# Where a decode kernel's first weights land: wq whole and first, w_down on 128 partitions

## The chip, the cores and the metric

One Trainium2 chip, one of its cores. The time is device time in microseconds (us) of one execution. Before the change it was 2534.05 us, the median of three runs (2532.77 to 2534.06). The core has TensorE (matmuls, called PE in the profile), VectorE (DVE), ScalarE (ACT), GpSimd (POOL), SyncE (SP), which here issues nearly all transfers, and 16 DMA engines that move the data between HBM and SBUF, the on-chip memory of 128 partitions.

## The reference, cut to what matters

One token is decoded. A 32-head attention over a cache of 65,536 positions and a SwiGLU feed-forward read the same input x, and a sigmoid gate mixes their results. Everything is bf16.

```python
def _A_ref(x, k_cache, v_cache, wq, wo):          # x [1,1,512], caches [1,32,65536,128]
    q = (x @ wq).reshape(B, Sq, H, Dh).transpose(0, 2, 1, 3)
    scores = jnp.einsum("bhqd,bhkd->bhqk", q, k_cache) * (Dh ** -0.5)
    p = softmax(scores, axis=-1)
    o = jnp.einsum("bhqk,bhkd->bhqd", p, v_cache)
    return o.transpose(0, 2, 1, 3).reshape(B, Sq, H * Dh) @ wo

def _B_ref(x, w_gate, w_up, w_down):              # F = 1792
    return (silu(x @ w_gate) * (x @ w_up)) @ w_down

g = sigmoid((x * gate_w).sum(-1, keepdims=True))
return g * _A_ref(...) + (1 - g) * _B_ref(...)
```

The caches are 2 x 32 x 65536 x 128 x 2 bytes, 1073.7 MB. wq and wo have 4.19 MB each, w_gate, w_up and w_down 1.835 MB each.

## The kernel before, in words

A head's K and V are cut into G = 4 tiles of 128 partitions with 128 rows of 128 numbers each (NB = 128), so a tile has 32 KB in every partition, 4 MB in all. There are N = 128 tiles of K and as many of V.

**The ring.** All large loads go into five slots of 32 KB per partition (SLOTS = 5). `take` (line 81) hands out the slot that was freed first, `give` (line 88) puts one back. A load into a slot waits until whatever read the slot's last content is done. SP issues the loads in program order, so a load that waits holds up those behind it in SP's queue. The slots lie in SBUF behind the pool of constants; as built, the first begins at byte 30,976 of each partition.

**The scores.** `products` (line 245) multiplies a K tile by the head's query on VectorE (line 254) and folds it by halves (line 258), to 64 numbers a row for the first head (FIRST) and to 32 for the others (WIDTH). `scores` (line 263) sums the rest on TensorE with identity matmuls (line 267), which frees the K slot; `fold` (line 277) takes the last four numbers together. At a head's end come the row maximum (line 285), the exponentials (line 294), and `values` (line 316), 32 matmuls for a V tile (line 322), which frees the V slot.

**The queries.** `queries(g)` (line 146) makes the queries of four heads with four matmuls against wq (line 149) and copies them to SBUF on ScalarE (line 156).

**The beginning, written out by hand (lines 99 to 124 and 380 to 420).** SP first issues the first four heads' part of wq (0.5 MB, rows of 1 KB) into a tile of the `wo_pool`, then K0, K1 and K2. The other 3.5 MB of wq (rows of 7 KB) have the fourth slot. A one-element GpSimd copy (line 381) writes into that slot once the first queries are done, and the load waits for it:

```python
queries(0)
nc.gpsimd.tensor_copy(out=wq_t[0:1, 0:1], in_=q_bc[0:1, 0:1])
nc.sync.dma_start(out=wq_rest, in_=wq_rows[:, :, QW:])
```

K0's slot then takes w_gate and w_up, with K3 issued between them (lines 387 to 389). K1's slot takes w_down, K2's takes V0, and wq's takes K4. w_down lies on 64 partitions, 28 KB in each, and comes in eight transfers of 8 partitions (line 402), six ahead of K4 and two behind it:

```python
firsts = (0, 1, 2, 3, 32, 33, 34, 35)
part = slice(firsts[i], firsts[i] + 29, 4)
```

**The loop (line 433).** From n = 4 on, each step loads one K tile and one V tile, multiplies and sums K tile n and weights V tile v. The list `steps` lets V fall behind K by up to LAG = 8 tiles after n = 40. In step n = 4 the feed-forward is finished (`feed_forward_mid`, line 214, and `feed_forward_out`, line 223): since w_down lies on 64 partitions, two matmuls (line 227) turn the hidden vector from 128 x 14 to 64 x 28, ScalarE copies it (line 231), and 28 matmuls of 512 columns (line 233) follow. Then w_down's slot is free for K6.

**The end.** The last V tile comes in six pieces, and half of wo in four (line 169), behind it in SP's queue.

Of the kernel before, what the change touches and what calls it, by code (L numbers as in the profile page):

```python
# [8 lines left out]
ACT = mybir.ActivationFunctionType  # L9
ALU = mybir.AluOpType  # L10
AXIS = mybir.AxisListType
P = 128
# [3 lines left out]
NB = 128  # L16
# [17 lines left out]
def kernel(  # L34
# [14 lines left out]
    nc = tc.nc  # L49
    bf16 = mybir.dt.bfloat16  # L50
    f32 = mybir.dt.float32

    _, H, Sk, Dh = A_k_cache.shape
    D = A_x.shape[2]
    F = B_w_gate.shape[1]
    KT = D // P
    FT = F // P
    G = Sk // (NB * P)
    NBH = Sk // P
    N = H * G  # L60
    QG = 4
# [3 lines left out]
    consts = ctx.enter_context(tc.tile_pool(name="consts", bufs=1))  # L65
# [3 lines left out]
    wo_pool = ctx.enter_context(tc.tile_pool(name="wo_pool", bufs=2))  # L69
# [3 lines left out]
    psum_m = ctx.enter_context(tc.tile_pool(name="psum_m", bufs=2, space=bass.MemoryType.PSUM))  # L73
# [7 lines left out]
    def take(name):  # L81
        slot = free.pop(0)
        held[name] = slot
        return ring.tile(
            [P, NB * Dh], bf16, name=name.split(".")[0], tag=f"slot{slot}"
        )

    def give(name):
        free.append(held.pop(name))

    xT = consts.tile([P, KT], bf16, name="xT")
    gwT = consts.tile([P, KT], bf16, name="gwT")
    with nc.allow_non_contiguous_dma(reason="small"):
# [1 line left out]
        nc.scalar.dma_start(out=gwT, in_=gate_w.rearrange("(p t) -> p t", t=KT))  # L95

    QW = QG * Dh
    wq_rows = A_wq.rearrange("(p t) f -> p t f", t=KT)
    wq_first = wo_pool.tile([P, KT, QW], bf16, name="wq_first", tag="wo_sb")
    nc.sync.dma_start(out=wq_first, in_=wq_rows[:, :, :QW])  # L100

    K_tiles, V_tiles, S_tiles, F_tiles, P_tiles, O_tiles = {}, {}, {}, {}, {}, {}

    def load(dst, cache, n, name, cuts=(0, NB), slot=None):
        h, g = divmod(n, G)
        t = take(f"{name}.{n}") if slot is None else slot
        view = t.rearrange("p (j d) -> p j d", d=Dh)
        src = cache[0, h, g * NB * P : (g + 1) * NB * P, :].rearrange("(p j) d -> p j d", j=NB)
        for a, b in zip(cuts[:-1], cuts[1:]):
            nc.sync.dma_start(out=view[:, a:b, :], in_=src[:, a:b, :])  # L110
        dst[n] = view

    def load_k(n):
        load(K_tiles, A_k_cache, n, "K_t")
# [1 line left out]
    def load_v(n):  # L116
        load(V_tiles, A_v_cache, n, "V_t", V_CUTS.get(N - n, (0, NB)))

    load_k(0)
    load_k(1)  # L120
    load_k(2)
    wq_t = take("wq_t.0")
    wq_rest = wq_t[:, : KT * (H * Dh - QW)].rearrange("p (t f) -> p t f", t=KT)
    K3_t = take("K_t.3")

    ident_f = consts.tile([P, P], f32, name="ident_f")
    make_identity(nc, ident_f[:])
    ident_b = consts.tile([P, P], bf16, name="ident_b")
# [4 lines left out]
    q_bc = consts.tile([P, H * Dh], bf16, name="q_bc")  # L133
# [12 lines left out]
    def queries(g):  # L146
        qg_ps = psum_m.tile([P, QW], f32, name="qg_ps", tag="misc")
        for t in range(KT):
            nc.tensor.matmul(
                qg_ps,  # L150
                lhsT=X_bc[:, t, :],
                rhs=wq_first[:, t, :] if g == 0 else wq_rest[:, t, (g - 1) * QW : g * QW],
                start=(t == 0),
                stop=(t == KT - 1),
            )
        nc.scalar.activation(out=q_bc[:, g * QW : (g + 1) * QW], in_=qg_ps, func=ACT.Copy)
# [34 lines left out]
    def gate_sum():  # L191
        xg = consts.tile([P, KT], f32, name="xg")
        nc.vector.tensor_tensor(out=xg, in0=xT, in1=gwT, op=ALU.mult)
        xs = consts.tile([P, 1], f32, name="xs")
        nc.vector.tensor_reduce(out=xs, in_=xg, axis=AXIS.X, op=ALU.add)
        return xs

    def gate_exp(xs):
        g_ps = psum_m.tile([P, 1], f32, name="g_ps", tag="misc")
        nc.tensor.matmul(g_ps, lhsT=ones_f, rhs=xs, start=True, stop=True)  # L200
        eg2 = consts.tile([P, 1], f32, name="eg2")
        nc.scalar.activation(out=eg2, in_=g_ps, func=ACT.Exp, scale=-1.0)
        return eg2

    def gate_value(eg2):
        nc.vector.tensor_scalar_add(eg2, eg2, 1.0)
        nc.vector.reciprocal(gval, eg2)
        rest = consts.tile([1, 1], f32, name="rest")
        nc.vector.tensor_scalar(
            out=rest, in0=gval[0:1, :], scalar1=-1.0, scalar2=1.0, op0=ALU.mult, op1=ALU.add  # L210
        )
        return rest
# [9 lines left out]

    def feed_forward_out(hT, rest):
        b_ps = psum_m.tile([1, D], f32, name="b_ps", tag="misc")
        h_ps = psum_m.tile([HP, GT], f32, name="h_ps", tag="misc")
        for r in range(2):
            nc.tensor.matmul(
                h_ps[:, r * FT : (r + 1) * FT], lhsT=ident_b[:, r::2], rhs=hT, start=True, stop=True
            )
        h2 = consts.tile([HP, GT], bf16, name="h2")  # L230
        nc.scalar.activation(out=h2, in_=h_ps, func=ACT.Copy)  # L231
        for t in range(GT):
            nc.tensor.matmul(  # L233
                b_ps, lhsT=h2[:, t : t + 1], rhs=wd_sb[:, t, :], start=(t == 0), stop=(t == GT - 1)
            )
        nc.scalar.activation(out=b_sb, in_=b_ps, func=ACT.Copy, scale=rest)
        for i, a in enumerate(a_ps):
            nc.tensor.matmul(  # L238
                a, lhsT=ones_f[0:1, 0:1], rhs=b_sb[:, i * HD : (i + 1) * HD], start=True, stop=False
            )  # L240

    def width_of(n):
        return FIRST if n < G else WIDTH

    def products(n, a=0, b=NB):
        h = n // G
        K = K_tiles[n][:, a:b, :]
        qb = q_bc[:, h * Dh : (h + 1) * Dh]
        q_rep = bass.AP(
            tensor=qb.tensor,  # L250
            offset=qb.offset,
            ap=[list(qb.ap[0]), [0, b - a], [1, Dh]],
        )
        yield nc.vector.tensor_tensor(out=K, in0=K, in1=q_rep, op=ALU.mult)  # L254
        half = Dh
        while half > width_of(n):
            half //= 2
            yield nc.vector.tensor_tensor(  # L258
                out=K[:, :, 0:half], in0=K[:, :, 0:half], in1=K[:, :, half : 2 * half],
                op=ALU.add,  # L260
            )

    def scores(n):
        S = F_tiles[n] = psum_s.tile([P, NB, QUAD], f32, name="S_ps")
        width = width_of(n)
        for c in range(0, width, QUAD):
            nc.tensor.matmul(  # L267
                S,
                lhsT=ident_b,
                rhs=K_tiles[n][:, :, c : c + QUAD],  # L270
                start=(c == 0),
                stop=(c == width - QUAD),
            )
        del K_tiles[n]
        give(f"K_t.{n}")

    def fold(n):
        h, g = divmod(n, G)
        if g == 0:
            S_tiles[h] = small.tile([P, NBH], f32, name="S_sb")  # L280
        nc.vector.tensor_reduce(  # L281
            out=S_tiles[h][:, g * NB : (g + 1) * NB], in_=F_tiles.pop(n), axis=AXIS.X, op=ALU.add
        )
# [90 lines left out]
    def score_tile(n):  # L374
        for _ in products(n):
            pass
        if n:
            fold(n - 1)

    queries(0)  # L380
    nc.gpsimd.tensor_copy(out=wq_t[0:1, 0:1], in_=q_bc[0:1, 0:1])
    nc.sync.dma_start(out=wq_rest, in_=wq_rows[:, :, QW:])
    score_tile(0)
    scores(0)
    gu_t = take("gu_t.0")
    wgu_sb = gu_t[:, : 2 * KT * F].rearrange("p (w t f) -> p w t f", w=2, t=KT)
    nc.sync.dma_start(out=wgu_sb[:, 0], in_=B_w_gate.rearrange("(p t) f -> p t f", t=KT))
    load(K_tiles, A_k_cache, 3, "K_t", slot=K3_t)
    nc.sync.dma_start(out=wgu_sb[:, 1], in_=B_w_up.rearrange("(p t) f -> p t f", t=KT))
    score_tile(1)  # L390
    xs = gate_sum()
    scores(1)
    wd_t = take("wd_t.0")
    HP = P // 2
    GT = F // HP
    wd_sb = wd_t[:HP, : GT * D].rearrange("p (t n) -> p t n", t=GT)
    wd_rows = B_w_down.rearrange("(p t) n -> p t n", t=GT)
    firsts = (0, 1, 2, 3, 32, 33, 34, 35)

    def load_wd(i):  # L400
        part = slice(firsts[i], firsts[i] + 29, 4)
        nc.sync.dma_start(out=wd_sb[part], in_=wd_rows[part])

    for i in range(6):
        load_wd(i)
    for g in range(1, H // QG):
        queries(g)
    give("wq_t.0")
    eg2 = gate_exp(xs)
    load_k(4)  # L410
    load_wd(6)
    load_wd(7)
    score_tile(2)
    rest = gate_value(eg2)
    scores(2)
    load_v(0)
    ff = feed_forward_in()
# [15 lines left out]
    for n, v in steps:  # L433
# [22 lines left out]
        if n == G:  # L456
            hT = feed_forward_mid(*ff)
# [7 lines left out]
        if n == G:  # L465
            feed_forward_out(hT, rest)
            give("wd_t.0")
# [49 lines left out]
```

## Time and profile before

| | |
|---|---|
| median of three runs | 2534.05 us (2532.77 to 2534.06) |
| the profiled execution | 2534.41 us, its span 2532.6 us |
| TensorE busy | 1533.7 us (61%) |
| VectorE busy | 2083.7 us (82%) |
| read from HBM | 1087.64 MB, 429 GB/s over the span |
| a transfer of a K tile | 4096 KB, 35.3 us from issue to landing (median) |
| mean granted TensorE clock | 0.772 of full speed |

The profile page has one execution, in 40 slices of 63.3 us where it shows rates. "DMA share" is the mean busy share of the 16 DMA engines in a stretch; a packet counts with its whole size where it ends, so that over 2 or 3 us the share can pass 1. A row of the timeline has start, length, engine, line, operation, its tiles, and in brackets how long the engine was idle before and what ended that. SPq stands for SP's queue of issues: such a row starts when the issue does, not when data moves. Packet and landing records, where they are named, are the trace's lists of DMA packets (start, length, size) and of the 16 completion counts that each transfer posts, one for each DMA engine.

### The profile page before, as it was taken

To read this page: it belongs to the slowest core of one execution; us is meant where nothing else is said; L and a number is where in the kernel's file an instruction comes from. 1 tells how busy PE (TensorE), PEld (TensorE's weight loads), DVE (VectorE), ACT (ScalarE), POOL (GpSimd) and SP (SyncE) were. 2 spreads that over 40 slices of the span, in tenths; PEclk is the share of its full clock that TensorE was granted. 3 is DMA by queue.
4 is the path that set the end of the run, shared out by engine and by line. 5 is a ranking of instruction groups with operands and counts; after the bars stand their busy time and mean duration, and the time that the engine had idled before them with its cause. 6 is when DMAs were issued, how large, how long until landed. Compare 5 with 4: busy or idle time off the path is not lost.

```text
span 2532.6 us, 13195 instructions
## 1 busy us (share of the span) xinstructions
PE 1533.7 (61%) x5786; PEld 581.6 (23%) x5786; DVE 2083.7 (82%) x744; ACT 77.7 (3%) x208; POOL 0.9 (0%) x7
## 2 busy tenths in 40 slices
PE   4656656665566555555665566556656665665569
PEld 1222222222222112222222122222222221222223
DVE  7788888888887999988888888888888888888860
ACT  1000000000000000000000000000000000000000
POOL 0000000000000000000000000000000000000000
PEclk9777777777777787787777777777777777777779
DMA  9999999999999999999999999999999999999998
GB/s 412 418 431 433 435 432 430 434 433 432 431 433 434 431 433 434 432 431 434 433 432 433 434 432 432 435 431 432 432 434 432 431 435 433 431 434 433 432 432 351
DMA packets 43915, 1088.49 MB, mean 430 GB/s; under 512 B 4753, under 2 KB 9362, under 8 KB 10258
## 3 DMA queue, kind: packets, MB, share of 16 engines
q1 hardware_dynamic: 43570, 1087.65, 99.7%
q8 instruction: 45, 0.74, 0.1%
q14 instruction: 12, 0.10, 0.0%
q10 hardware_dynamic: 288, 0.00, 0.0%
HBM read 1087.64 MB, written 0.00 MB: 429 GB/s over the span
## 4 chain that ended last, share of the span: by engine, by line
DMA 71%; PE 23%; DVE 4%; issue 1%; ACT 0%; SPq 0%; DVEq 0%
DMA V_t<-in_A_v_cache_dram 63%; PE O_ps L322 21%; DMA K_t<-in_A_k_cache_dram 8%; DVE K_t L254 3%; DVE K_t L258 1%; PE S_ps L267 1%; DMA wo_late<-in_A_wo_dram 0%; PE b_ps L233 0%; DVE S_sb L281 0%; DVE m L287 0%; PE oh_ps L351 0%; PE a_ps L238 0%; ACT P_sb L300 0%; PE a_ps L365 0%; PE mT_ps L291 0%
## 5 line engine op out<-in xcount | busy, mean ns | idle before, releaser
L322 PE MATMUL O_ps<-V_t,P_sb 128*4 128x512 bf16 x4094 | 1154.5, 452 | 663.5 <-DMA V_t<-in_A_v_cache_dram 663.5
L254 DVE TENSOR_TENSOR K_t<-K_t,q_bc 128x16384 bf16<-128x16384 bf16 (+1 forms) x159 | 1117.2, 7026 | 357.9 <-DMA K_t<-in_A_k_cache_dram 346.7
L258 DVE TENSOR_TENSOR K_t<-K_t 128x8192 bf16<-128x8192 bf16 (+1 forms) x314 | 859.7, 2738 | 8.6
L322 PEld LDWEIGHTS <-P_sb 128*4 128x4 bf16 x4094 | 393.0, 97 | 1405.1 <-issue 1064.1
L267 PE MATMUL S_ps<-K_t,ident_b 128*128 128x512 bf16 x1056 | 263.3, 393 | 100.6 <-DVE K_t L258 100.6
L267 PEld LDWEIGHTS <-ident_b 128*128 128x128 bf16 x1056 | 98.0, 101 | 248.0 <-issue 158.0
L291 PE MATMUL mT_ps<-diag,ones_f 128*128 128x128 f32 x64 | 24.5, 483 | 150.1 <-ACT diag L289 150.1
L351 PE MATMUL oh_ps<-ident_f,O_sb 4*128 4x1 f32 x256 | 55.5, 334 | 74.5 <-ACT O_sb L335 74.5
L281 DVE TENSOR_REDUCE S_sb<-S_ps 128x128 f32<-128x512 f32 x128 | 87.5, 683 | 4.9 <-PE S_ps L267 4.9
L289 ACT ACTIVATE diag<-ident_f,m 128x128 f32<-128x128 f32 x32 | 12.8, 401 | 2118.7 <-DVE m L287 2118.7
L351 PEld LDWEIGHTS oh_ps<-ident_f,O_sb 4*128 4x128 f32 x256 | 52.8, 301 | 84.1 <-ACT O_sb L335 82.9
L291 PEld LDWEIGHTS mT_ps<-diag,ones_f 128*128 128x128 f32 x64 | 15.2, 295 | 166.7 <-ACT diag L289 166.7
L484 DVE CAST out_sb<-a_ps 1x256 bf16<-1x256 f32 x1 | 0.4, 412 | 56.6 <-PE a_ps L365 56.6
L300 ACT ACTIVATE P_sb<-S_sb,bias 128x512 bf16<-128x512 f32 x32 | 23.1, 722 | 1.0
L287 DVE TENSOR_REDUCE m<-S_sb 128x1 f32<-128x512 f32 x32 | 22.0, 686 | 1.1
L335 ACT ACTIVATE O_sb<-O_ps 4x512 f32<-4x512 f32 x32 | 18.3, 572 | 129.2 <-PE O_ps L322 129.2
L313 DVE RECIPROCAL recip<-tot_ps 128x1 f32<-128x1 f32 x32 | 5.1, 158 | 13.0 <-PE tot_ps L308 13.0
L308 PEld LDWEIGHTS tot_ps<-rowsum,ones_f 128*128 128x128 f32 x64 | 9.5, 188 | 14.0 <-issue 14.0
L233 PE MATMUL b_ps<-wd_t,h 64*1 64x512 bf16 x28 | 12.1, 625 | 0.3 <-ACT h L231 0.3
L308 PE MATMUL tot_ps<-rowsum,ones_f 128*128 128x1 f32 x64 | 12.2, 260 | 0.0
L358 ACT ACTIVATE oT<-oh_ps,rg 128x1 bf16<-128x1 f32 x32 | 8.4, 263 | 65.0 <-PE oh_ps L351 65.0
L296 DVE TENSOR_REDUCE top<-mT_ps 128x1 f32<-128x128 f32 x32 | 9.1, 284 | 1.0 <-PE mT_ps L291 1.0
(47 smaller groups left out, 75.2 us busy)
## 6 DMA issues: line engine op xcount, KB each, us to landing
K_t<-in_A_k_cache_dram SPq DMA_DIRECT2D x128, 4096.0 KB, 35.3
V_t<-in_A_v_cache_dram SPq DMA_DIRECT2D x125, 4096.0 KB, 28.0
V_t<-in_A_v_cache_dram SPq DMA_DIRECT2D x4, 2048.0 KB, 31.1
wq_t<-in_A_wq_dram SPq DMA_DIRECT2D x1, 3584.0 KB
V_t<-in_A_v_cache_dram SPq DMA_DIRECT2D x3, 1024.0 KB
wo_sb<-in_A_wo_dram SPq DMA_DIRECT2D x4, 512.0 KB, 38.8
gu_t<-in_B_w_gate_dram SPq DMA_DIRECT2D x1, 1792.0 KB
gu_t<-in_B_w_up_dram SPq DMA_DIRECT2D x1, 1792.0 KB
```

Of the source, the lines that this page charges most:

```text
L254: yield nc.vector.tensor_tensor(out=K, in0=K, in1=q_rep, op=ALU.mult)
L258: yield nc.vector.tensor_tensor(out=K[:, :, 0:half], in0=K[:, :, 0:half], in1=K[:, :, half : 2 * half], op=ALU.add,)
L267: nc.tensor.matmul(S, lhsT=ident_b, rhs=K_tiles[n][:, :, c : c + QUAD], start=(c == 0), stop=(c == width - QUAD),)
L281: nc.vector.tensor_reduce(out=S_tiles[h][:, g * NB : (g + 1) * NB], in_=F_tiles.pop(n), axis=AXIS.X, op=ALU.add)
L287: nc.vector.tensor_reduce(out=m, in_=S_tiles[h], axis=AXIS.X, op=ALU.max)
L289: nc.scalar.activation(out=diag, in_=ident_f, func=ACT.Copy, scale=m)
L291: nc.tensor.matmul(mT_ps, lhsT=ones_f, rhs=diag, start=True, stop=True)
L300: nc.scalar.activation(out=P_tiles[h], in_=S_tiles[h], func=ACT.Exp, bias=bias, scale=scale, accum_out=rowsum[:, h : h + 1],)
L308: nc.tensor.matmul(tot_ps, lhsT=ones_f, rhs=rowsum[:, h : h + 1], start=True, stop=True)
L322: nc.tensor.matmul(O_tiles[h], lhsT=P_tiles[h][:, g * NB + j : g * NB + j + 4], rhs=V_tiles[n][:, j : j + 4, :], start=(g == 0 and j == 0) ...
L335: nc.scalar.activation(out=O_sb, in_=O_tiles.pop(h), func=ACT.Copy)
L351: nc.tensor.matmul(oh_ps, lhsT=O_sb[:, c * Dh : (c + 1) * Dh], rhs=ident_f[0:4, c : c + 1], start=(c == 0 and not turned), stop=(c == 3),)
```

## The change

Three things are edited.

- **wq** is taken whole (4 MB, rows of 32 KB) into the first slot of the ring, as the first load. K0 to K3 follow in the other four. All eight groups of queries are made before any product. The GpSimd copy, `wq_first` and the `slot` argument of `load` go. wq's slot takes w_gate and w_up, K0's takes w_down, K1's takes K4 and K2's takes V0.
- **w_down** lies on 128 partitions, 14 KB in each, in one transfer. The hidden vector is used as it stands, with 14 matmuls; the two turning matmuls, the copy and the tile `h2` go. The gate's small operations (`gate_sum`, `gate_exp`, `gate_value`) come one tile earlier.
- **A tile of 64 bytes**, `fill`, that nothing reads or writes, is added to the constants ahead of the ring. As built, the ring begins at byte 30,976 of each partition, with the 64 bytes of `h2` gone and those of `fill` there.

```diff
+    consts.tile([P, 32], bf16, name="fill")
...
-    wq_rows = A_wq.rearrange("(p t) f -> p t f", t=KT)
-    wq_first = wo_pool.tile([P, KT, QW], bf16, name="wq_first", tag="wo_sb")
-    nc.sync.dma_start(out=wq_first, in_=wq_rows[:, :, :QW])
+    wq_t = take("wq_t.0")
+    nc.sync.dma_start(out=wq_t, in_=A_wq.rearrange("(p t) f -> p (t f)", t=KT))
+    wq_sb = wq_t.rearrange("p (t f) -> p t f", t=KT)
...
-    load_k(0)
-    load_k(1)
-    load_k(2)
-    wq_t = take("wq_t.0")
-    wq_rest = wq_t[:, : KT * (H * Dh - QW)].rearrange("p (t f) -> p t f", t=KT)
-    K3_t = take("K_t.3")
+    for n in range(G):
+        load_k(n)
...
     def feed_forward_out(hT, rest):
         b_ps = psum_m.tile([1, D], f32, name="b_ps", tag="misc")
-        h_ps = psum_m.tile([HP, GT], f32, name="h_ps", tag="misc")
-        for r in range(2):
-            nc.tensor.matmul(
-                h_ps[:, r * FT : (r + 1) * FT], lhsT=ident_b[:, r::2], rhs=hT, start=True, stop=True
-            )
-        h2 = consts.tile([HP, GT], bf16, name="h2")
-        nc.scalar.activation(out=h2, in_=h_ps, func=ACT.Copy)
-        for t in range(GT):
-            nc.tensor.matmul(
-                b_ps, lhsT=h2[:, t : t + 1], rhs=wd_sb[:, t, :], start=(t == 0), stop=(t == GT - 1)
+        for t in range(FT):
+            nc.tensor.matmul(
+                b_ps, lhsT=hT[:, t : t + 1], rhs=wd_sb[:, t, :], start=(t == 0), stop=(t == FT - 1)
             )
...
-    queries(0)
-    nc.gpsimd.tensor_copy(out=wq_t[0:1, 0:1], in_=q_bc[0:1, 0:1])
-    nc.sync.dma_start(out=wq_rest, in_=wq_rows[:, :, QW:])
-    score_tile(0)
-    scores(0)
+    for g in range(H // QG):
+        queries(g)
+    give("wq_t.0")
     gu_t = take("gu_t.0")
     wgu_sb = gu_t[:, : 2 * KT * F].rearrange("p (w t f) -> p w t f", w=2, t=KT)
-    nc.sync.dma_start(out=wgu_sb[:, 0], in_=B_w_gate.rearrange("(p t) f -> p t f", t=KT))
-    load(K_tiles, A_k_cache, 3, "K_t", slot=K3_t)
-    nc.sync.dma_start(out=wgu_sb[:, 1], in_=B_w_up.rearrange("(p t) f -> p t f", t=KT))
-    score_tile(1)
+    for w, rows in enumerate((B_w_gate, B_w_up)):
+        nc.sync.dma_start(out=wgu_sb[:, w], in_=rows.rearrange("(p t) f -> p t f", t=KT))
+    score_tile(0)
     xs = gate_sum()
-    scores(1)
-    wd_t = take("wd_t.0")
-    HP = P // 2
-    GT = F // HP
-    wd_sb = wd_t[:HP, : GT * D].rearrange("p (t n) -> p t n", t=GT)
-    wd_rows = B_w_down.rearrange("(p t) n -> p t n", t=GT)
-    firsts = (0, 1, 2, 3, 32, 33, 34, 35)
-
-    def load_wd(i):
-        part = slice(firsts[i], firsts[i] + 29, 4)
-        nc.sync.dma_start(out=wd_sb[part], in_=wd_rows[part])
-
-    for i in range(6):
-        load_wd(i)
-    for g in range(1, H // QG):
-        queries(g)
-    give("wq_t.0")
+    scores(0)
     eg2 = gate_exp(xs)
+    wd_t = take("wd_t.0")
+    wd_sb = wd_t[:, : FT * D].rearrange("p (t n) -> p t n", t=FT)
+    nc.sync.dma_start(out=wd_sb, in_=B_w_down.rearrange("(p t) n -> p t n", t=FT))
+    score_tile(1)
+    rest = gate_value(eg2)
+    scores(1)
     load_k(4)
-    load_wd(6)
-    load_wd(7)
     score_tile(2)
-    rest = gate_value(eg2)
     scores(2)
     load_v(0)
```

More of the change, by code (lines that the diff above doesn't have):

```diff
@@ L97, with load @@
     QW = QG * Dh
-    wq_rows = A_wq.rearrange("(p t) f -> p t f", t=KT)
-    wq_first = wo_pool.tile([P, KT, QW], bf16, name="wq_first", tag="wo_sb")
-    nc.sync.dma_start(out=wq_first, in_=wq_rows[:, :, :QW])
+    wq_t = take("wq_t.0")
+    nc.sync.dma_start(out=wq_t, in_=A_wq.rearrange("(p t) f -> p (t f)", t=KT))
+    wq_sb = wq_t.rearrange("p (t f) -> p t f", t=KT)
     K_tiles, V_tiles, S_tiles, F_tiles, P_tiles, O_tiles = {}, {}, {}, {}, {}, {}
-    def load(dst, cache, n, name, cuts=(0, NB), slot=None):
+    def load(dst, cache, n, name, cuts=(0, NB)):
         h, g = divmod(n, G)
-        t = take(f"{name}.{n}") if slot is None else slot
+        t = take(f"{name}.{n}")
         view = t.rearrange("p (j d) -> p j d", d=Dh)
@@ L151, in queries @@
                 lhsT=X_bc[:, t, :],
-                rhs=wq_first[:, t, :] if g == 0 else wq_rest[:, t, (g - 1) * QW : g * QW],
+                rhs=wq_sb[:, t, g * QW : (g + 1) * QW],
                 start=(t == 0),
@@ L378, in score_tile @@
             fold(n - 1)
-    queries(0)
-    nc.gpsimd.tensor_copy(out=wq_t[0:1, 0:1], in_=q_bc[0:1, 0:1])
-    nc.sync.dma_start(out=wq_rest, in_=wq_rows[:, :, QW:])
-    score_tile(0)
-    scores(0)
+    for g in range(H // QG):
+        queries(g)
+    give("wq_t.0")
     gu_t = take("gu_t.0")
     wgu_sb = gu_t[:, : 2 * KT * F].rearrange("p (w t f) -> p w t f", w=2, t=KT)
-    nc.sync.dma_start(out=wgu_sb[:, 0], in_=B_w_gate.rearrange("(p t) f -> p t f", t=KT))
-    load(K_tiles, A_k_cache, 3, "K_t", slot=K3_t)
-    nc.sync.dma_start(out=wgu_sb[:, 1], in_=B_w_up.rearrange("(p t) f -> p t f", t=KT))
+    for w, rows in enumerate((B_w_gate, B_w_up)):
+        nc.sync.dma_start(out=wgu_sb[:, w], in_=rows.rearrange("(p t) f -> p t f", t=KT))
+    score_tile(0)
+    xs = gate_sum()
+    scores(0)
+    eg2 = gate_exp(xs)
+    wd_t = take("wd_t.0")
+    wd_sb = wd_t[:, : FT * D].rearrange("p (t n) -> p t n", t=FT)
+    nc.sync.dma_start(out=wd_sb, in_=B_w_down.rearrange("(p t) n -> p t n", t=FT))
     score_tile(1)
-    xs = gate_sum()
+    rest = gate_value(eg2)
     scores(1)
-    wd_t = take("wd_t.0")
-    HP = P // 2
-    GT = F // HP
-    wd_sb = wd_t[:HP, : GT * D].rearrange("p (t n) -> p t n", t=GT)
-    wd_rows = B_w_down.rearrange("(p t) n -> p t n", t=GT)
-    firsts = (0, 1, 2, 3, 32, 33, 34, 35)
-    def load_wd(i):
-        part = slice(firsts[i], firsts[i] + 29, 4)
-        nc.sync.dma_start(out=wd_sb[part], in_=wd_rows[part])
-    for i in range(6):
-        load_wd(i)
-    for g in range(1, H // QG):
-        queries(g)
-    give("wq_t.0")
-    eg2 = gate_exp(xs)
     load_k(4)
-    load_wd(6)
-    load_wd(7)
     score_tile(2)
-    rest = gate_value(eg2)
     scores(2)
```

## The prediction

> **What bounds the kernel now.** I read the page first: engines, DMA rate, queues. VectorE is busy 82% and TensorE 61%, while the transfers run at one rate from the first slices to the last.
>
> ```profile
> PE 1533.7 (61%) x5786; PEld 581.6 (23%) x5786; DVE 2083.7 (82%) x744; ACT 77.7 (3%) x208; POOL 0.9 (0%) x7
> GB/s 412 418 431 433 435 432 430 434 433 432 431 433 434 431 433 434 432 431 434 433 432 433 434 432 432 435 431 432 432 434 432 431 435 433 431 434 433 432 432 351
> q1 hardware_dynamic: 43570, 1087.65, 99.7%
> q8 instruction: 45, 0.74, 0.1%
> HBM read 1087.64 MB, written 0.00 MB: 429 GB/s over the span
> ```
>
> 1087.65 MB at 433 GB/s are 2512 us of a 2532.6 us span. So the bound is the 16 DMA engines, and only three things can move the time: the bytes' efficiency, engines without work, and uneven work among the 16. The second view is the table of stretches, with the DMA share and GB/s as last columns.
>
> ```profile
> 13.40:23.00 9.60, 0.00 (x0) 0.00 (x0) 8.20 (x1) 0.00 (x0) 0.00 (x0) 1.00 1.01 437
> 99.50:101.50 2.00, 1.23 (x4) 0.20 (x3) 1.61 (x1) 0.68 (x1) 0.00 (x0) 0.50 0.76 246
> 104.00:2510.00 2406.00, 1462.79 (x5432) 550.10 (x5430) 2005.91 (x709) 67.31 (x186) 0.00 (x0) 0.77 1.00 433
> 2520.00:2523.00 3.00, 2.72 (x13) 1.01 (x12) 0.00 (x0) 0.00 (x0) 0.00 (x0) 1.00 0.49 143
> 2523.00:2526.00 3.00, 2.54 (x23) 1.42 (x20) 0.00 (x0) 0.59 (x1) 0.00 (x0) 1.00 0.76 252
> 2526.00:2529.00 3.00, 2.94 (x27) 2.18 (x28) 0.00 (x0) 0.26 (x1) 0.00 (x0) 1.00 0.09 33
> ```
>
> All engines are full from 104 to 2510 us. Around 100 us and in the last 10 us some are empty while others still work: the work is uneven. The timeline shows where that begins. w_down goes out in eight pieces of 8 partitions; six are queued between K3 and K4.
>
> ```profile
> 46.38 4.19 SPq L402 DMA_DIRECT2D wd_t<-in_B_w_down_dram  x6
> 56.97 8.69 DVE L254 TENSOR_TENSOR K_t<-K_t,q_bc 128x16384 bf16<-128x16384 bf16 x1 [1.00 <-DMA K_t<-in_A_k_cache_dram]
> 57.01 0.34 SPq L110 DMA_DIRECT2D K_t<-in_A_k_cache_dram  x1
> 78.44 4.42 DVE L254 TENSOR_TENSOR K_t<-K_t,q_bc 128x8192 bf16<-128x8192 bf16 x1 [7.72 <-issue]
> 100.10 0.33 SPq L110 DMA_DIRECT2D K_t<-in_A_k_cache_dram  x1
> 2509.15 14.16 SPq L169 DMA_DIRECT2D wo_late<-in_A_wo_dram  x4
> ```
>
> VectorE starts K3 when it lands (56.97) and K4 when that lands (78.44): 21.5 us. In between the queue carried w_up (1.835 MB, 4.24 us at 433 GB/s), six pieces of w_down (1.376 MB) and K4 (4.194 MB, 9.69 us). On 16 engines the pieces take 3.2 us, 17.1 in all; on eight 6.4, 20.3 in all. So the pieces run on eight engines. The packet records agree: 64 packets of 28,672 B, 1.062 us each, eight to an engine: 8.5 us of work on eight engines, none on the others.
>
> The landing records (one per engine and transfer) show the effect: K1's 16 parts land within 0.6 us, V0's in two groups 8.5 us apart, V123's (2484.8 us) over 14 us. The leading eight ran dry once near 100 us, waiting for the issue at 100.10, which gave back about 2.7 us. The rest of the growth is instruction fetches: each of the 45 packets of q8 holds one engine up by 1.4 us. They go round eight engines, two of them among those with w_down, so the last engine carries w_down and six fetches. It is never idle from 2.2 us to the end, and every tile waits for it. Its work is the time.
>
> **The change, part by part.** (1) w_down on 128 partitions: 128 packets of 14,336 B. Gate and up have that form: 0.535 us a packet, 4.31 us from landing to landing (42.96 to 47.27). The last engine's w_down falls from 8.50 to 4.31 us: -4.2. Bounds: 0, if the engines even out by themselves, and -8.5, if w_down vanished from that engine. I take -4.2, counted on the engine that ends last.
>
> (2) wq whole: in place of 512 packets of 1,024 B (46 ns) and 512 of 7,168 B (272 ns), 10.2 us per engine, 128 of 32,768 B (1.213 us), 9.7 us. That is -0.47 by packets alone; by landings wq's rest took 8.94 us behind K2, with 1.47 for the first part, against 9.66 for a whole tile: -0.75, which holds the gaps too. I take -0.75.
>
> (3) The ring. Two halves cancel: the 64 bytes of the new filler stand where h2 stood, and as built the slots start at byte 30,976 (121 x 256) in both kernels. 0 us, no wait, no instruction.
>
> (4) The start is reordered: K0 lands 8.2 us later (14.70 + 9.66 - 1.47 = 22.9). Does any engine run dry? wq lands at 13.2. 32 query matmuls (0.43 us cold for some eight, then 0.88 a group with the 0.60 us copies beside them) end at 22, so q is there with K0. A first-head tile takes VectorE 13.07 us (14.80 to 27.87), besides 0.61 for a fold and 0.35 and 0.55 for the gate's small operations: products start at 23.0, 36.4, 50.7, 64.4; the 16 score matmuls (5.0 to 5.9 us) end at 41.1, 54.9, 69.1, 83.2. SP's queue in its new order, the time the engines want each transfer against its issue:
> gate and up: 50.6 against 22; w_down (slot of K0): 59.2 against 41.2; K4 (slot of K1): 63.5 against 54.9; V0 (slot of K2): 73.2 against 69.1; K5 (slot of gate and up, 112 matmuls, 6.83 us): 82.8 against 76; V1: 92.5 against 83.3; K6 (slot of w_down): 102.2 against 94; V2: 113.3 against 105.
> From the first issue at 0.74 to the first packet at 2.22 are 1.5 us, so V0 is the tightest, with 2.6 us to spare. Nothing runs dry: 0 us. If VectorE were x us later than this, it would cost x - 2.6. K4 lands at 74.5, VectorE reaches it at 78.2, so from step 4 on everything stands as before.
>
> (5) The second matmul stage: two matmuls, a copy of 0.19 us and 14 of 28 matmuls at 0.43 us go: 6.6 us of TensorE, 88 to 100 us. It lies beside transfers; its only reader is the release of w_down's slot, which moves K6 from 100.1 to 94. At 100.1 and 1.5 us for the first packet K6 would still be in time for 102.2. The POOL copy that held SP (4.4 us) goes with K1 and K2 queued behind it: 0.
>
> Sum: -4.2 - 0.75 = -4.95 us. The profiled execution took 2534.41 (span 2532.6 and 1.8 around it), 0.36 above the median of the runs: 2529.46 for one like it, 2529.1 against the median. That is 0.195% less; 0.2% (5.07 us, 2528.98) is about what a measurement of this kernel can tell from no change, so the forecast stands on the border.
>
> **The rivals.** *The uneven share was hidden.* If the engines drew on one shared rate, the ones ahead would leave theirs to the ones behind, and w_down's placing would cost nothing: only wq's -0.75, 2533.3. Against it: with engines empty from 99.5 to 101.5 us the rate fell to 246 GB/s at a share of 0.76, and did not stay at 433.
> The Trainium skill, DMA: Bandwidth & Descriptors, Specifications, puts HBM at about 358 GB/s for a core, below the engines' 435; by that rule HBM binds and this rival would hold. The 433 GB/s of 104 to 2510 us disagree.
>
> *Engines in step are slower* (the other side). Today's offset of 8.5 us and more among the engines ends, so 16 streams of 32 KB rows walk HBM in step for the whole run. 246 tiles follow V0. At 20 ns a tile the gain is gone, from 41 ns the kernel is slower by over 0.2%; at 60 ns, the widest difference between two tiles' spacings in this trace (9.65 and 9.71): 2529.1 + 14.8 = 2543.9. Against it: in step (13.4 to 23.0 us) the rate is 437, and K0, K1, K2 land 9.67 and 9.65 us apart, against 9.66 to 9.71 late in the run.
> [...]
>
> *One fetch less on the last engine.* Which engine ends last is decided by fetches of 1.4 us. One of the three runs lies 1.3 us below the others. With five instead of six: 2527.7. Against it: five engines now carry six alike.
>
> **How the numbers follow.** Forecast 0.62 (2528.3 to 2530.0, half on either side of 2529.0 within rounding), one fetch less 0.14, hidden 0.13, in step slower 0.11. Faster by over 0.2%: 0.31 + 0.14 = 0.45; within: 0.31 + 0.13 = 0.44; slower 0.11. The range takes the fewer fetch below (2527.2) and the hidden case above (2533.6) and leaves out the slower one.
>
> **What would show it.** The stretch around 100 us has a DMA share of 1.0, and w_down's packets take 4.3 us from w_up to K4. V0 is issued at about 69 and K4's products start near 78. From 2520 us on, fewer engines are empty. The last issue of wo_late comes some 5 us earlier. Wrong it would be with a share below 0.95 between 60 and 120 us (a slot came late), a rate under 432 in the long stretch (in step is slower), or an end no earlier though w_down takes half (the share was hidden).

## The result, and the profile after

The changed kernel takes 2529.11 us (median of 19 runs, 2528.88 to 2529.41), the kernel before 2534.0 us (19 runs beside them, 2532.46 to 2535.21). The ratio is 0.9981, with a 95% interval of 0.9975 to 0.9987: 4.9 us less, or 0.19%, which is clear of noise but under the 0.2% that the prediction took for its border. The forecast was 2529.1; that it is met to within 0.1 us is luck, since the terms below were measured no closer than some 0.2.

The page of the changed kernel: the engines as busy as before, the same bytes, a slightly shorter span, and DMA engines that reach their rate in the second slice (435, where it was 418).

```profile
span 2527.4 us, 13150 instructions
PE 1523.3 (60%) x5770; PEld 579.9 (23%) x5770; DVE 2083.6 (82%) x744; ACT 77.6 (3%) x207; POOL 0.7 (0%) x6
GB/s 415 435 431 431 434 434 432 433 432 431 434 431 435 432 431 433 433 432 434 432 433 432 432 433 434 433 432 432 433 434 433 432 432 432 435 434 432 431 432 370
q1 hardware_dynamic: 42674, 1087.65, 99.9%
q8 instruction: 45, 0.74, 0.1%
```

Stretches, DMA share and GB/s last. First the kernel before, then the changed one:

```profile
98.00:104.00 6.00, 5.23 (x13) 1.17 (x12) 4.11 (x1) 0.68 (x1) 0.00 (x0) 0.50 0.89 350
```

```profile
98.00:104.00 6.00, 5.22 (x25) 2.07 (x24) 6.00 (x1) 0.00 (x0) 0.00 (x0) 1.00 1.01 437
104.00:2500.00 2396.00, 1447.11 (x5375) 545.30 (x5375) 2002.52 (x709) 67.34 (x186) 0.00 (x0) 0.77 1.00 433
2515.00:2518.00 3.00, 2.74 (x13) 1.01 (x12) 0.00 (x0) 0.00 (x0) 0.00 (x0) 1.00 0.73 249
2518.00:2521.00 3.00, 2.54 (x23) 1.59 (x22) 0.00 (x0) 0.59 (x1) 0.00 (x0) 1.00 0.84 296
2521.00:2524.00 3.00, 2.95 (x27) 2.15 (x27) 0.00 (x0) 0.26 (x1) 0.00 (x0) 1.00 0.35 118
```

No engine is empty near 100 us any more. The long stretch runs at the same 433 GB/s. The last three stretches lie 5 us earlier than the last three of the prediction's table, because the kernel ends that much earlier: fewer engines stand empty in them than before (0.73, 0.84 and 0.35, where it had 0.49, 0.76 and 0.09). The timeline of SP's issues and of the products of K0 and K4 in the changed kernel:

```profile
0.74 0.41 SPq L101 DMA_DIRECT2D wq_t<-in_A_wq_dram  x1
1.20 2.26 SPq L112 DMA_DIRECT2D K_t<-in_A_k_cache_dram  x4
22.82 8.69 DVE L245 TENSOR_TENSOR K_t<-K_t,q_bc 128x16384 bf16<-128x16384 bf16 x1 [14.03 <-DMA K_t<-in_A_k_cache_dram]
41.83 0.33 SPq L384 DMA_DIRECT2D wd_t<-in_B_w_down_dram  x1
55.32 0.33 SPq L112 DMA_DIRECT2D K_t<-in_A_k_cache_dram  x1
69.20 0.33 SPq L112 DMA_DIRECT2D V_t<-in_A_v_cache_dram  x1
77.57 4.42 DVE L245 TENSOR_TENSOR K_t<-K_t,q_bc 128x8192 bf16<-128x8192 bf16 x1
92.40 0.33 SPq L112 DMA_DIRECT2D K_t<-in_A_k_cache_dram  x1
2503.92 14.13 SPq L167 DMA_DIRECT2D wo_late<-in_A_wo_dram  x4
```

VectorE starts 8 us later and is level with the old kernel when it reaches K4 (77.57, before 78.44). V0's last part lands at 85.30 us by the landing records, where it was 90.15: the gain is there by then. The last issue of wo_late ends at 2518.05, where it was 2523.31. The spread of a tile's 16 landings near the end is 8.7 us, where it was 14.0.

### The profile page after: what moved, and what is told of

It reads as the page before. It is cut to its first block, busy times and chain, and to the rows that moved or that the text cites. A ratio compares the mean times of both kernels' runs of the same rounds, so it can differ in the third digit from the quotient of the medians.

```text
span 2527.4 us, 13150 instructions
## 1 busy us (share of the span) xinstructions
PE 1523.3 (60%) x5770; PEld 579.9 (23%) x5770; DVE 2083.6 (82%) x744; ACT 77.6 (3%) x207; POOL 0.7 (0%) x6
## 4 chain that ended last, share of the span: by engine, by line
DMA 71%; PE 22%; DVE 6%; issue 0%; ACT 0%; SPq 0%; DVEq 0%
DMA V_t<-in_A_v_cache_dram 65%; PE O_ps L313 21%; DMA K_t<-in_A_k_cache_dram 6%; DVE K_t L245 3%; DVE K_t L249 2%; PE S_ps L258 1%; DMA wo_late<-in_A_wo_dram 0%; DVE S_sb L272 0%; PE oh_ps L342 0%; DVE m L278 0%; ACT P_sb L291 0%; PE a_ps L356 0%; PE mT_ps L282 0%; ACT O_sb L326 0%; DVE top L287 0%
## 5 line engine op out<-in xcount | busy, mean ns | idle before, releaser
L147 PE MATMUL qg_ps<-wq_t,X_bc 128*128 128x512 bf16 x32 | 8.8, 443 | 13.0 <-DMA wq_t<-in_A_wq_dram 13.0
```

## The experiments

The theory: the DMA engine that ends last sets the time, by the packets that it alone carries. The rivals: the uneven share is hidden, the new order of the start is what counts, the ring's alignment counts. Times are medians of 9 to 11 runs; beside them the kernel before gave 2533.99 to 2534.15. Three dots in an edit stand for lines left out.

### w_down alone

```diff
 # the kernel before
+    consts.tile([P, 32], bf16, name="fill")
... (feed_forward_out as in the change: 14 matmuls, no h2)
-    wd_sb = wd_t[:HP, : GT * D].rearrange("p (t n) -> p t n", t=GT)
...
-    for i in range(6):
-        load_wd(i)
+    wd_sb = wd_t[:, : FT * D].rearrange("p (t n) -> p t n", t=FT)
+    nc.sync.dma_start(out=wd_sb, in_=B_w_down.rearrange("(p t) n -> p t n", t=FT))
...
-    load_wd(6)
-    load_wd(7)
```

> The kernel before with w_down alone changed: one transfer to 128 partitions, 14 matmuls, the filler in place of h2; wq stays in two parts. Theory (the engine that ends last sets the time): that engine's w_down falls from 8.50 to 4.31 us, so the time falls by 4.2 to about 2529.8 us, and all engines stay full around 100 us. Rival (the uneven share is hidden, engines share one rate): no change, 2534.0 us.

Measured: 2529.87 us (2529.6 to 2530.18), 4.2 less than the kernel before. The stretch near 100 us:

```profile
98.00:104.00 6.00, 4.46 (x22) 1.76 (x20) 6.00 (x1) 0.00 (x0) 0.00 (x0) 1.00 1.01 437
```

All engines are full there, with wq still in two parts and K0 early. This kernel also leaves out the second matmul stage, and K6 is issued at 91.64 in place of 100.10. But V0's last part lands at 86.14, where it was 90.15, so the gain was there before that stage could matter. What remains is w_down's spread over the engines, and the rival of the hidden share falls: the bytes were the same.

### wq alone

```diff
 # the changed kernel
-    consts.tile([P, 32], bf16, name="fill")
... (feed_forward_out as in the kernel before, with h2)
-    wd_sb = wd_t[:, : FT * D].rearrange("p (t n) -> p t n", t=FT)
-    nc.sync.dma_start(out=wd_sb, in_=B_w_down.rearrange("(p t) n -> p t n", t=FT))
+    wd_sb = wd_t[:HP, : GT * D].rearrange("p (t n) -> p t n", t=GT)
...
+    for i in range(8):
+        part = slice(firsts[i], firsts[i] + 29, 4)
+        nc.sync.dma_start(out=wd_sb[part], in_=wd_rows[part])
```

> The changed kernel with w_down put back on 64 partitions, in eight pieces of 8, all ahead of K4; wq stays whole and first. Theory: only wq's gain of 0.5 to 0.75 us is left, about 2533.3 us, and the landings of V tiles are split in two groups again, some 8.5 us apart. Rival (the new order of the start is what gains): the time stays at 2529.1 us. If K0's later landing cost something that w_down's gain covered, it would be over 2534.0 us.

Measured: 2533.52 us (2531.97 to 2534.16), 0.6 less than the 2534.1 of the kernel before beside it; the interval of the ratio (0.999 to 1.0008) does not tell that from nothing. Against the changed kernel, w_down back on 64 partitions costs 4.4; against w_down alone, wq whole and first saves 0.8 (2529.87 to 2529.11, runs that do not overlap). The order of the start is not the gain, and K0's later landing costs nothing that shows.

One sign that was expected did not come. V0's two groups land 4.4 us apart, not 8.5, and near the end the spread of a tile's landings is 10.0 us, not 14.0. The eight pieces held SP, so that K4 was issued only at 61.31 (55.32 in the changed kernel), and the engines without w_down stood empty for 2.4 to 3.8 us near 62 us by the packet records:

```profile
56.00:66.00 10.00, 2.46 (x6) 0.82 (x6) 9.97 (x4) 0.00 (x0) 0.00 (x0) 0.65 0.86 342
```

That made the spread smaller and not the time: the last part of V0 lands at 89.77 against 85.30 in the changed kernel, and the last part of wo_late at 2528.47 against 2523.95, both 4.5 later. What counts is when the last engine is done, not how far the others are ahead.

### The filler

```diff
 # the changed kernel
-    consts.tile([P, 32], bf16, name="fill")
```

> The changed kernel without the 64-byte filler: every ring slot begins 64 bytes earlier, 192 past a multiple of 256. Theory as predicted says nothing of this case, since both kernels had aligned slots; by bounds it costs nothing (2529.1 us) or, an estimate, one more piece of 256 bytes for each row of 32 KB, 1 in 128, 0.8% of the time: about 2549 us. If it costs that, the transfers' rate falls below 433 GB/s in the long stretch.

Measured: 2539.34 us (2539.18 to 2539.53): 10.2 more than with the filler, and 5.2 more than the kernel before (ratio 1.0022, interval 1.0013 to 1.003). The long stretch of this kernel:

```profile
104.00:2500.00 2396.00, 1440.18 (x5329) 541.86 (x5329) 2002.88 (x709) 67.35 (x186) 0.00 (x0) 0.76 1.00 431
```

431 in place of 433 GB/s, with all engines full. A row of 32 KB takes 1.215 us in the median of the packet records in place of 1.213, and a tenth of the rows 1.222 or more. In the mean it is 4 ns more (1.2178 against 1.2138), about 8 us over some 2030 rows on each engine; the packets of the instruction fetches are longer too (1.07 against 0.93 us). The 10.2 us are about half of the upper bound of the expectation. So the 64 bytes are worth twice the rest of the change; in this change they stand for h2's 64 bytes, which had done the same.

### Half a step of alignment

```diff
 # the changed kernel
-    consts.tile([P, 32], bf16, name="fill")
+    consts.tile([P, 96], bf16, name="fill")
```

> The changed kernel with a filler of 192 bytes in place of 64: the ring slots begin 128 bytes past a multiple of 256. The kernel without the filler (192 past a multiple) took 10.2 us more. If what counts is a multiple of 256, this one takes about as much more, 2539 us; if 128 is enough, 2529.1 us.

Measured: 2539.11 us (2538.76 to 2539.34), 10.0 more than the changed kernel, and the same 431 GB/s:

```profile
104.00:2500.00 2396.00, 1439.12 (x5323) 541.31 (x5322) 2001.67 (x709) 67.09 (x185) 0.00 (x0) 0.76 1.00 431
```

128 bytes are not enough. The Trainium skill, DMA: Bandwidth & Descriptors, How a descriptor splits into AXI transactions, says that a transaction starts at a multiple of 256 bytes and that a piece which starts elsewhere pays for the bytes below its start. These two runs agree with a step of 256, for the place that a load writes to: the slots of the changed kernel, at 121 x 256, are not at a multiple of 512. By that rule 192 bytes past a step should cost half as much again as 128; here both cost the same.

### A useless load of 127 and of 128 rows

```diff
 # the changed kernel, behind w_down's load; rows = 127 and 128
+    nc.sync.dma_start(
+        out=wd_t[:rows, FT * D : FT * D + 1024],
+        in_=B_w_gate.rearrange("(p t) f -> p (t f)", t=KT)[:rows, :1024],
+    )
```

> The changed kernel with one useless load behind w_down: 127 partitions of 2 KB (0.26 MB) into the unused part of its slot. If 127 rows cannot be divided among engines, all 127 packets of 84 ns lie on one engine, 10.7 us. Theory: the last engine is now that one or still one of those with six fetches, 8.6 us behind an engine with none; so the time rises by 2 us if the engine has no fetches and by up to 10.7 if it has six: 2531 to 2540 us. Rival (shared rate): 0.26 MB at 433 GB/s, 0.6 us: 2529.7 us.

> The same useless load with 128 partitions of 2 KB in place of 127. Eight packets of 84 ns on each of 16 engines, 0.67 us. Theory and rival alike: about 2529.8 us, 0.6 to 0.7 above the changed kernel. It tells whether what the load of 127 rows costs comes from its bytes and its place in the queue or from its engine.

Measured: 2532.59 us with 127 rows (2532.34 to 2532.8), 2529.64 with 128 (2529.44 to 2529.97). One row less costs 3.0 us more, so which engines a load lies on counts and not its bytes. But it does not count by the way that was expected. The load lies on one engine (it posts one landing beside the one that comes at once), and the rise was expected at 2 us if that engine has no fetches. It has none: by the landing records one engine is 8.2 us behind the first from K4 to the end of the run, with no step in between, while others rise past it to 8.9. So that engine does not end last, and yet the time is 3.5 above the changed kernel's. What costs time is seen in SP's timeline of the kernel with 127 rows (start, duration, queue and line):

```profile
42.65 0.32 SPq L385 DMA_DIRECT2D wd_t<-in_B_w_gate_dram  x1
55.76 8.48 SPq L112 DMA_DIRECT2D K_t<-in_A_k_cache_dram  x1
```

and in the stretch that follows, by windows, which had 418 GB/s in the changed kernel:

```profile
66.00:76.00 10.00, 10.00 (x121) 7.87 (x120) 9.96 (x2) 0.00 (x0) 0.00 (x0) 0.67 0.97 337
```

K4's issue, 0.33 us otherwise, took 8.48 us with 127 packets ahead of it on one engine. By the packet records the other 15 then stood empty for 0.5 to 1.3 us near 65 us. After that they were busy (0.97), but K4's rows took 1.55 us in the median, up to 2.35, in place of 1.213, as long as the 127 packets were under way. Both together made K4's first part land at 77.5 us in place of 74.0, and these 3.5 us are the price; the slower rows are the larger part of it. Why the rows were slow was not tried.

### VectorE late on purpose

```diff
 # the changed kernel
+    late = late_pool.tile([P, H * Dh], bf16, name="late")
+    for _ in range(4):
+        nc.vector.tensor_tensor(out=late, in0=q_bc, in1=q_bc, op=ALU.mult)
     score_tile(0)
```

> The changed kernel with four useless multiplications of 4096 columns on VectorE (about 2.2 us each, 8.7 us) ahead of the first product. It tests the spare time that the prediction gave the start. Theory: VectorE is 8.7 us late, V0 is issued at about 78 instead of 69.2, its first packet comes 1.5 us later where the engines want it at 73: they stand empty for about 6 us in all, and the time rises by as much, to 2535 us. Rival (the ring's backlog takes it up, or K4 and V0 have more room than worked out): under 1 us, 2529 to 2530 us.

Measured: 2536.04 us (2535.29 to 2536.92), 6.9 more. V0 is issued at 78.18, and the engines are short of work just where the prediction's table had the least room:

```profile
56.00:66.00 10.00, 5.23 (x16) 1.88 (x16) 9.93 (x6) 0.00 (x0) 0.00 (x0) 0.68 0.95 381
66.00:76.00 10.00, 2.87 (x7) 0.97 (x7) 9.97 (x4) 0.00 (x0) 0.00 (x0) 0.66 0.86 374
76.00:86.00 10.00, 8.83 (x122) 7.69 (x121) 9.96 (x2) 0.41 (x2) 0.00 (x0) 0.84 0.74 287
```

By the packet records all engines stood empty twice, for 0.8 to 2.3 us before K4's first packets near 65 us and for 1.6 to 4.0 us before V0's near 79. The start's cover is real and thin: of 8.7 us of delay, 6.9 come out at the end, where about 6 were expected. The new order costs nothing, because VectorE is just in time.

### Uneven on purpose

```diff
 # the changed kernel
-    nc.sync.dma_start(out=wd_sb, in_=B_w_down.rearrange("(p t) n -> p t n", t=FT))
+    CUT, FEW = 9, 102
+    nc.sync.dma_start(out=wd_sb[:, :CUT], in_=wd_rows[:, :CUT])
+    nc.sync.dma_start(out=wd_sb[:FEW, CUT:], in_=wd_rows[:FEW, CUT:])
+    nc.sync.dma_start(out=wd_sb[FEW:, CUT:], in_=wd_rows[FEW:, CUT:])
```

> The changed kernel with w_down's last 5 of 14 columns of rows loaded apart: 102 partitions, which six engines share (102 = 6 x 17), and the other 26. The aim is to give more to engines that have no instruction fetches. Theory: if the six are engines without fetches, the last engine's w_down falls from 4.3 to about 3.1 us and the time by about 1.1, to 2528.0 us, with a narrower spread of landings at the end. If two of them have fetches, these end last with 4.28 x 9/14 + 3.25 + 0.4 = 6.4 us of w_down, 2531 us. Rival (shared rate): 2529.1 us.

Measured: 2533.72 us (2532.95 to 2535.14), 4.6 more than the changed kernel: a miss, worse than both numbers. The landing records show two reasons. Six engines are behind by 3.3 to 4.0 us from K4 on, and one of them takes fetches (10.4 us behind at the end, the last). And the packets are slow: those of 5,120 B on w_down's last columns took 0.37 us in the median, though the shortest took 0.196, and K4's rows on the other engines took 1.5 to 2.9 us between 62 and 70 us, in place of 1.213. Between 56 and 76 us all engines are busy at 353 GB/s; the changed kernel had 430 there.

```profile
56.00:76.00 20.00, 12.39 (x128) 8.80 (x128) 19.93 (x5) 0.00 (x0) 0.00 (x0) 0.63 1.02 353
```

Why these packets are slow was not tried. The load of 127 rows had the same beside its small packets. The eight-partition pieces of the kernel before were not slow (1.062 us for 28,672 B), and K4's rows beside them took 1.213.

### More fetches, fewer fetches

```diff
 # the changed kernel, more: the same sums in two halves from n = 4 on
+        cuts = (0, NB) if n < G else (0, NB // 2, NB)
+        for j, k in zip(cuts[:-1], cuts[1:]):
...
-                S,
+                    S[:, j:k, :],
-                rhs=K_tiles[n][:, :, c : c + QUAD],
+                    rhs=K_tiles[n][:, j:k, c : c + QUAD],
```

> The changed kernel with each score matmul of the later heads cut in two halves of 256 columns: the same arithmetic in 992 more matmuls, so about 8 more instruction fetches of 16 KB (53 in place of 45). Theory: the fetches go round eight engines, so each of these gets one more, and the engine that ends last is held up 1.4 us longer: 2530.5 us, with a spread of landings of some 10.1 us at the end in place of 8.7. Rival (fetches cost no more than their 0.13 MB, shared by all): below 0.3 us, 2529.4 us or less.

```diff
 # the changed kernel, fewer: VectorE folds to 16 and 8 in turn
-        return FIRST if n < G else WIDTH
+        return FIRST if n < G else WIDTH // 4 if n % 2 else WIDTH // 2
```

> The changed kernel with more folding on VectorE (to 16 and 8 numbers a row in turn, in place of 32) for the heads after the first: 620 fewer score matmuls, 1240 fewer rows of PE's program, some 5 fetches less (40 in place of 45), so five on the last engine in place of six. VectorE gets about 1.2 us more on even tiles and 1.9 on odd ones, 190 us in all, 90% busy. Theory: 1.4 us less, 2527.7 us, if the DMA engines stay full. Rival (VectorE becomes the bound where K runs ahead of V, 740 to 1000 us): the rate falls below 433 GB/s there and the time rises, to 2531 us or more.

Measured: 2530.42 us with more (2530.32 to 2530.61), 2527.86 with fewer (2527.66 to 2528.01). The pages of the two, more fetches first:

```profile
PE 1527.1 (60%) x6762; PEld 675.0 (27%) x6762; DVE 2083.2 (82%) x744; ACT 77.6 (3%) x207; POOL 0.7 (0%) x6
q8 instruction: 53, 0.87, 0.1%
```

```profile
PE 1399.8 (55%) x5150; PEld 523.8 (21%) x5150; DVE 2281.4 (90%) x961; ACT 77.6 (3%) x207; POOL 0.7 (0%) x6
q8 instruction: 40, 0.66, 0.1%
```

and the long stretch of the one with fewer:

```profile
104.00:2500.00 2396.00, 1325.52 (x4765) 490.11 (x4765) 2200.58 (x924) 67.38 (x186) 0.00 (x0) 0.75 1.00 433
```

With 53 fetches 1.3 us more, with 40 1.25 less; the landings' spread near the end is 10.2 and 5.0 us (8.7 in the changed kernel; 7.1 would be five fetches). In the kernel with fewer the engines that were ahead have also waited: by the packet records some stood empty for 2.3 to 3.1 us near 1088 us, before the V tile issued at 1086.42. The last landings tell the two effects apart. In the changed kernel the parts of the last V tile's last piece land from 2509.76 to 2518.50 us; with 53 fetches from 2509.52 to 2519.84, with 40 from 2512.16 to 2517.10. The first engine is as early as before with more fetches, and 2.4 us later with fewer; the time follows the last one in both. The 0.13 MB more or 0.08 MB less are 0.3 us at most at 433 GB/s. So the fetches on one engine set the end, each at about 1.3 us. The kernel with fewer is the fastest of all: it beats the changed kernel by 1.25 us and the kernel before by 0.24% (ratio 0.9976, interval 0.9967 to 0.9986), with VectorE at 90% of the span and the long stretch still at 433.

## Why the prediction was right, point by point

- **w_down, -4.2.** Right: alone 4.2 less, and put back 4.4 more. The engine that ends last has eight packets of 14,336 B in place of eight of 28,672; w_up to w_down took 4.22 us from landing to landing (60.38 to 64.60). The reading of the old trace that decided it, 21.5 us between K3 and K4, needed no packet records.
- **wq, -0.75.** Right: 0.8 less beside w_down alone, 0.6 in the noisier pair. The landings were nearer than the packets' 0.47. (The 1.47 us in that sum are not a landing but 32 packets of 46 ns.)
- **The ring, 0.** Right for this change, with both kernels at 30,976. What the prediction did not price is what the filler holds off, 10.2 us, the largest term met here.
- **The start, 0.** Right, and the table held: w_down issued at 41.83 (41.2 worked out), K4 55.32 (54.9), V0 69.20 (69.1), K6 92.40 (94). K4's products start at 77.57 (78.2). The delay of 8.7 us cost 6.9 where 8.7 - 2.6 = 6.1 was the rule.
- **The second matmul stage, 0.** Right as far as it shows: K6 was issued 7.7 us earlier, and no run takes this part by itself (w_down alone leaves the stage out too). But the whole difference, 90.15 to 85.30, stands at V0's last landing, before the stage ends, and the eight engines that stood empty near 101 us before were those ahead.
- **The rivals.** Hidden share: fell with w_down alone and with w_down put back; the useless loads do not bear on it, since what the 127 rows cost came by SP's held issue and slow rows. In step slower: fell, though it was not tried for the whole run. Rows of 32 KB take 1.213 us in the median between 110 and 300 us, where a tile's landings lie within 2 us of each other, and as long later, when fetches have drawn them apart to 8.7. One fetch less on the last engine: it did not occur in this change (45 fetches, all 19 runs within 0.6 us), but its price was right, as the runs with 53 and 40 show.
- **What would show it.** A share of 1.0 near 100 us holds over 6 us; over 2 us (99.5 to 101.5) the changed kernel shows 0.64 though no engine was empty, because packets are counted where they end. So 0.76 over 2 us, on which the prediction built in part, was too short a stretch; over 6 us the kernel before has 0.89, and the same reading.

## What to carry to other kernels

Where the DMA engines are full from end to end, count the work of each engine and not only the bytes: a load of few partitions or of a number that does not go evenly into 16 engines (here 127 lay on one, 102 on six), and instruction fetches, go to some engines alone, and the last one sets the time. Look at the spread of a transfer's landings among the engines: it shows what was uneven, but it also shrinks when the engines ahead wait, so go by the last landing. Keep what large transfers write to at multiples of 256 bytes, and ask after every small tile added or removed ahead of them whether it still holds.

## What was not expected

- An unaligned destination costs 0.4% of the whole run (10.2 us at 192 bytes past 256, 10.0 at 128), though nearly all bytes come in rows of 32 KB.
- With 127 packets waiting on one engine, SP's next issue took 8.48 us; the other 15 engines stood empty for 0.5 to 1.3 us, and the next tile's rows were slow, 1.55 us in place of 1.213. Together that cost 3.5 us for 0.26 MB.
- x, 1 KB in all, landed at 8.13 us in place of 2.49 once a load with 32 KB rows was issued beside it. VectorE's first copies started at 8.16, and wq landed only at 12.99, so nothing came of it here.
- Instruction fetches, 0.1% of the DMA engines' time in all, are worth about 1.3 us of the end for each on the engine that ends last, because they are not spread evenly: 40 in place of 45 made the fastest kernel.
